# Ordering the first score product of pairs 2 to 5 behind the values of the pair two places ahead

## The chip, the cores and the metric

The kernel runs on one core of a Trainium2 chip. The metric is the device time of one execution in microseconds (us), the median of several runs. The engines are TensorE (PE: matrix products, with the loads of its stationary operand shown apart as PEld), VectorE (DVE), ScalarE (ACT) and GpSimd (POOL); SyncE (SP) issues the DMA transfers. Each engine works through its own queue in order and waits on semaphores for the others.

## The reference

Attention with a compressive memory, followed by a feed-forward block with the Mish activation (names shortened):

```python
def _attn_ref(q, k, v, M_prev, z_prev, beta):          # q, k, v: (4, 8, 576, 64)
    scores = q @ k.T / sqrt(D), causal mask             # per batch and head
    a = exp(scores - scores.max(-1)); a /= a.sum(-1) + 1e-09
    local = a @ v
    q_p = where(q > 0, q, exp(q) - 1) + 1
    mem_out = (q_p @ M_prev) / (q_p @ z_prev + 1e-06)
    g = sigmoid(beta)                                   # per head
    return g * mem_out + (1 - g) * local

def reference(...):
    x = attn_out.transpose(0, 2, 1, 3).reshape(2304, 512)
    h = x @ w_in                                        # (512, 2048)
    return (h * tanh(softplus(h))) @ w_out              # (2048, 512)
```

All data are float32.

## The kernel before

**Pairs.** The 4 x 8 heads are handled as 16 pairs of heads, numbered 0 to 15. For each pair `load`, `load2` and `loadv` bring q and k transposed (`f`), q by rows (`qn`), `z` and `v` (with M_prev as its first 64 rows). Then come:

- `scores(p)`: the scores of both heads in four products, held in the list `banks`: `(4, 0, 288)` means query tile 4 against keys 0 to 287. The query tiles have up to 128 rows; tile 4 has all 576 keys and takes two products, `(4, 0, 288)` and `(4, 288, 576)`. Each product goes into a PSUM tile `s`; up to pair 3 there are two of these in turn, later one. DVE masks each piece and takes its running extreme in one instruction (`ttr`, L388, into the row buffer `w` and `mx`); the masking of keys 288 to 575 needs the extreme of keys 0 to 287. ACT takes the exponential with its sum (L395).
- `prep(p)`: the feature map of q (`p0`, exponential, `ph2`), its product with z on POOL and the denominators on DVE (L346 to L351).
- `norm(h)`: the reciprocal of the row sums (L431, L434), the scaling of the rows by it on POOL (L95), and the memory part, written into the same row buffer (POOL, L89).
- `transp(h)`: 15 transposes of 128 x 128 on PE (L459) in four groups, each evicted from PSUM into `at` (L112 on ACT, L114 on DVE, in turn: ACT, DVE, ACT, DVE).
- `av(p)`: the values, two groups of products (L487) into one accumulator `vps`; each group is copied by ACT (`xo`), and DVE subtracts the copy from the accumulator (`xl`, L89) to keep the rounding remainder. The second group needs the first one's accumulator free and all four evictions of both heads. `put` stores both to DRAM (`xs`).

**Weights.** The feed-forward weights are 16 column tiles, split into two float32r parts each. `split(...)` makes for one tile two conversions (`narrow`): a load into `raw`, a scaling on ACT (L93), on DVE L158, L164, L167 and L174, a cast on ACT, a subtraction on POOL and the last addition on DVE (L89, into `wi` or `wo`). Six tiles are converted in the attention part, after the scores of pairs 1 (one), 3 (one), 4 (two), 5 (one) and 6 (one); `raw` has one buffer there. The rest follows after the attention.

**Feed-forward part.** `steps_a` makes products for 9 blocks of 256 tokens with the six tiles already converted: L237 (input products, into `h`), Mish and a split, then L253 (output products, into `acc`). From pair 4 on some of these steps are put into the program behind each pair. `tail` does the remaining tiles for all tokens (L580, L597).

**What sets the order.** The program is written pair by pair, but the framework's scheduler deals the instructions out to the engine queues by priorities (`run(..., name)` shifts them by the table `OFF`) and by a timeline of its own. `order_after(ins, first)` (L99) adds a dependency without a semaphore: `ins` must stand behind `first` on its engine. `queued` (L105) uses it to keep the values of a pair in order; `before[0]` is the last values product so far.

Of the kernel before, what the change touches and what calls it, by code (L numbers as in the profile page):

```python
# [51 lines left out]
def f32(ap):  # L52
    return ap.bitcast(F32)
# [25 lines left out]
def attention_moe_kernel(ctx: ExitStack, tc: tile.TileContext, f_src, qn, vn, zz, beta, w_in, w_out, out):  # L79
    nc = tc.nc  # L80
# [7 lines left out]
    def tt(name, **kw):  # L88
        engines[ENG[name]].tensor_tensor(**kw)  # L89
# [7 lines left out]
    before = [None]  # L97

    def order_after(ins, first):  # L99
        tc.add_manual_dep(  # L100
            ins.ins, first.ins.name,
            mybir.DependencyInfo(mybir.DependencyClass.NoSync, mybir.DependencyReason.DATA), reason="order",
        )

    def queued(ins, chain):  # L105
        if chain:
            order_after(ins, before[0])
        before[0] = ins

    def copy(which, o, i):  # L110
        if which == "a":
            nc.scalar.copy(out=o, in_=i)  # L112
        elif which == "v":
            nc.vector.tensor_copy(out=o, in_=i)  # L114
        else:
            nc.gpsimd.tensor_scalar(out=o, in0=i, scalar1=1.0, scalar2=1.0, op0=ALU.mult, op1=ALU.mult)
# [161 lines left out]
    def attention():  # L278
# [9 lines left out]
        ps_v = st.enter_context(tc.tile_pool(name="ps_v", bufs=1, space=PS))  # L288

        pr = {}  # L290
        hd = {}
        turn = {"t": 0, "s": 0}
        early = ExitStack()
# [2 lines left out]
        def spare(p, order, pool, tag, shape):  # L296
            if p < EARLY and order[turn[tag] % len(order)] == "e":
                pool = ps_e
            turn[tag] += 1
            return pool.tile(shape, F32, tag=tag, name=tag)  # L300
# [56 lines left out]
        def scores(p):  # L357
            f = pr[p]["f"]
            gs = [hd.setdefault(2 * p + e, {}) for e in range(2)]
            ops = []  # L360

            def begin():
                for g in gs:
                    g["w"] = rp.tile([128, 1920], F32, tag="w", name="w")
                    g["mx"] = sp.tile([128, 6], F32, tag="mx", name="mx")
                    g["sm"] = sp.tile([128, 5], F32, tag="sm", name="sm")

            def mms(bank):
                ps = spare(p, SQ, ps_s, "s", [128, 2, 512])
                for e, g in enumerate(gs):  # L370
                    g["ps"] = ps[:, e]
                o = 0
                for m, a, b in bank:
                    n = b - a
                    q0 = QT[m][0]
                    for e, g in enumerate(gs):
                        le = slice(64 * e, 64 * e + 64)
                        nc.tensor.matmul(  # L378
                            g["ps"][:, o:o + n], f[le, 0, q0:q0 + 128], f[le, 1, a:b], start=True, stop=True
                        )  # L380
                    o += n

            def ttr(g, m, a, b, o):
                n = b - a
                c0 = 448 + (a - (QT[m][1] - 128)) if m else 448
                mx = g["mx"]
                acc = mx[:, 5:6] if b == 288 else mx[:, m:m + 1]
                nc.vector.tensor_tensor_reduce(  # L388
                    out=g["w"][:, WO[m] + D + a:WO[m] + D + b], in0=g["ps"][:, o:o + n], in1=mask[:, c0:c0 + n],
                    scale=-E_SC, scalar=3.0e38 if a == 0 else mx[:, 5:6], op0=ALU.add, op1=ALU.min, accum_out=acc,  # L390
                )

            def exp(g, m):
                row = g["w"][:, WO[m] + D:WO[m] + D + QT[m][1]]
                nc.scalar.activation(  # L395
                    out=row, in_=row, func=ACTF.Exp, scale=-1.0, bias=g["mx"][:, m:m + 1], accum_out=g["sm"][:, m:m + 1]
                )

            ops.append(begin)
            for bank in banks:  # L400
                ops.append(lambda bank=bank: mms(bank))
                for g in gs:
                    o = 0
                    for m, a, b in bank:
                        ops.append(lambda g=g, m=m, a=a, b=b, o=o: ttr(g, m, a, b, o))
                        o += b - a
                    for m, a, b in bank:
                        if b != 288:
                            ops.append(lambda g=g, m=m: exp(g, m))
            return ops  # L410
# [62 lines left out]
        def av(p):  # L473
            d = pr[p]
            at = [hd[2 * p + e]["at"] for e in range(2)]

            def mms(j):
                if j == 0:
                    d["xo"] = tp.tile([128, S], F32R, tag="xo", name="xo", bufs=2)
                    d["xl"] = tp.tile([128, S], F32, tag="xl", name="xl", bufs=2)  # L480
                q0, ops = AVJ[j]
                n = ops[0][2]
                ps = g_["v", j] = ps_v.tile([128, n], F32, tag="v", name="vps")
                last = len(ops) - 1
                for k, (t, a, b, gi, c) in enumerate(ops):
                    for e in (1, 0):
                        queued(nc.tensor.matmul(  # L487
                            ps[64 * e:64 * e + 64, a:b], d["v"][:, t, e], at[e][gi][:, c:c + b - a],
                            start=(k == 0), stop=(k == last),
                        ), k or e == 0)  # L490

            def cp(j):
                q0, n = AVJ[j][0], AVJ[j][1][0][2]
                xo = d["xo"][:, q0:q0 + n]
                copy("a", xo, g_["v", j][:])
                tt("xlo", out=d["xl"][:, q0:q0 + n], in0=g_["v", j][:], in1=f32(xo), op=ALU.subtract)

            def put():
                b, c = divmod(p, 4)
                nc.sync.dma_start(out=xs[b][:, 0, c, :], in_=f32(d["xo"][:]))  # L500
                nc.sync.dma_start(out=xs[b][:, 1, c, :], in_=d["xl"][:])

            g_ = {}
            ops = []
            for j in range(2):
                ops += [lambda j=j: mms(j), lambda j=j: cp(j)]
            return ops + [put]

        load(0)
        nc.sync.dma_start(out=gt[:, 2, :], in_=beta.to_broadcast([128, H]))  # L510
# [10 lines left out]
        for p in range(NP):  # L521
            load2(p)
            loadv(p)
            if p + 1 < NP:
                load(p + 1)
            run(scores(p), 'scores')
            run(prep(p), 'prep1')
            for _ in range(CV.get(p, 0)):
                run(split(wst, cp, nf), 'conv')
                nf += 1  # L530
            for e in range(2):
                run(norm(2 * p + e), 'norm')
                run(transp(2 * p + e), 'transp')
            run(av(p), 'av')
            if p == EARLY - 1:
                early.close()
                open_banks(st)
            if p >= P0:
                if (p - P0) % 4 == 0:
                    todo.extend(steps_a((p - P0) // 4))  # L540
                n = int(SPREAD * (p - P0 + 1)) - done[0]
                for _ in range(n):
                    run([todo.pop(0)], 'p1')
                done[0] += n
        st.close()

    def tail(mlist):
# [68 lines left out]
        st.close()  # L616

    attention()
    for k in range((NP - P0) // 4, (NA + 1) // 2):
        todo.extend(steps_a(k))  # L620
# [63 lines left out]
```

## Time and profile before

| | |
|---|---|
| median of 3 runs | 658.97 us (657.48 to 659.05) |
| profiled execution: time / span | 658.83 us / 657.0 us |
| PE busy, share of the span | 598.3 us, 91% |
| DVE busy | 334.2 us, 51% |
| ACT busy | 299.6 us, 46% |
| POOL busy | 170.3 us, 26% |
| mean granted PE clock | 0.966 of full |

The span runs from the first to the last instruction of the profiled execution; its time has 1.8 us more around it. Busy times are unions over an engine's instructions. The attention part takes the first 340 us or so, its second half mixed with feed-forward products; the last 250 us are feed-forward alone. A line with "[1.36 <-ACT xo L112]" means that the engine idled 1.36 us before it and that ACT's instruction at L112 which writes `xo` ended the wait.

### The profile page before, as it was taken

The page shows a single profiled execution, that of the slowest core. Times are in us where ns is not written, and L with a number is a line of the kernel's source. Part 1 is how long each engine was busy: PE and PEld are TensorE (multiplying, and loading weights), DVE is VectorE, ACT ScalarE, POOL GpSimd, SP SyncE. Part 2 cuts the span into 40 slices and gives each one's busy share as a digit, 9 for nine tenths or more (in the row PEclk, how much of TensorE's full clock was granted, in tenths as well). Part 3 has the DMA queues.
Part 4 walks back from the last instruction along what each step waited for, and adds up shares of the span by engine and source line. Part 5 has one row for each costly group of instructions (what it writes and reads, how often), then busy time and mean ns, then how long its engine had stood idle before and what let it go on. Part 6 is the DMA issues. An engine that isn't in the chain of part 4 may idle for free.

```text
span 657.0 us, 9863 instructions
## 1 busy us (share of the span) xinstructions
PE 598.3 (91%) x3488; PEld 470.3 (72%) x3488; DVE 334.2 (51%) x900; ACT 299.6 (46%) x688; POOL 170.3 (26%) x260
## 2 busy tenths in 40 slices
PE   3578868989988999989998999999999999999997
PEld 2345535767755877668887978888888888888886
DVE  4989887884575664635237888920311211121121
ACT  3677645866665775746244544621222222222221
POOL 3697885565435444414000000000000000000000
PEclk9579976999998999999998999999999999999999
DMA  6345566314545324421157666404302220430220
GB/s 227 98 137 159 191 208 213 127 58 144 167 149 187 97 86 129 155 105 58 50 178 245 215 235 208 128 1 128 111 19 71 90 95 1 129 128 1 64 97 32
DMA packets 50913, 80.86 MB, mean 123 GB/s; under 512 B 8112, under 2 KB 26544, under 8 KB 50864
## 3 DMA queue, kind: packets, MB, share of 16 engines
q1 hardware_dynamic: 50864, 80.24, 37.6%
q8 instruction: 27, 0.44, 0.3%
q14 instruction: 22, 0.18, 0.1%
HBM read 61.35 MB, written 18.87 MB: 122 GB/s over the span
## 4 chain that ended last, share of the span: by engine, by line
PE 50%; DMA 5%; DVE 2%; ACT 2%; issue 1%; POOL 1%; SPq 0%; DVEq 0%; ACTq 0%
PE o L597 19%; PE h L580 19%; PE h L237 5%; PE acc L253 4%; DMA raw<-in_w_in_dram 3%; PE vps L487 2%; PE t L459 2%; DMA part<-ob 1%; PE s L378 1%; POOL w L95 0%; DMA qn<-in_qn_dram 0%; DVE ws L174 0%; DVE wa L164 0%; ACT w L395 0%; ACT wa L93 0%
## 5 line engine op out<-in xcount | busy, mean ns | idle before, releaser
L89 DVE TENSOR_TENSOR g<-u,g 128x512 fp32r<-128x512 f32 (+1 forms) x77 | 50.7, 666 | 190.2 <-ACT g L112 190.1
L580 PE MATMUL h<-xb,wi 128*128 128x512 f32 (+1 forms) x600 | 134.8, 368 | 0.0
L597 PE MATMUL o<-wo,g 128*128 128x512 f32 x540 | 133.8, 390 | 0.0
L219 ACT ACTIVATE u<-h 128x512 f32<-128x512 f32 (+1 forms) x77 | 42.8, 569 | 180.9 <-PE h L580 168.5
L580 PEld LDWEIGHTS h<-xb,wi 128*128 128x128 f32 x600 | 106.0, 188 | 19.6
L597 PEld LDWEIGHTS o<-wo,g 128*128 128x128 f32 x540 | 100.6, 188 | 20.3
L95 POOL TENSOR_SCALAR w<-w,rc 128x64 f32<-128x64 f32 (+4 forms) x160 | 95.3, 617 | 72.8 <-ACT w L395 31.9
L395 ACT ACTIVATE w<-w,mx 128x576 f32<-128x576 f32 (+4 forms) x160 | 88.3, 553 | 31.0 <-DVE mx L388 30.4
L378 PE MATMUL s<-f 64*128 64x288 f32 (+4 forms) x384 | 69.2, 472 | 35.9 <-DVE mx L388 29.6
L237 PE MATMUL h<-xb,wi 128*128 128x256 f32 x648 | 93.5, 292 | 4.6 <-ACT u L219 4.6
L237 PEld LDWEIGHTS h<-xb,wi 128*128 128x128 f32 x648 | 83.7, 194 | 9.4 <-ACT u L219 5.4
L459 PE MATMUL t<-ident,w 128*128 128x128 f32 x480 | 77.1, 290 | 8.7 <-ACT at L112 5.9
L253 PE MATMUL acc<-wo,g 128*128 128x512 f32 x324 | 82.0, 396 | 0.6 <-ACT u L219 0.6
L378 PEld LDWEIGHTS s<-f 64*128 64x128 f32 x384 | 35.8, 209 | 62.2 <-DVE mx L388 37.5
L459 PEld LDWEIGHTS t<-ident,w 128*128 128x128 f32 x480 | 54.8, 146 | 27.6 <-issue 10.2
L253 PEld LDWEIGHTS acc<-wo,g 128*128 128x128 f32 x324 | 58.9, 188 | 12.7 <-ACT u L219 0.8
L487 PE MATMUL vps<-at,v 128*64 128x256 f32 (+2 forms) x512 | 62.2, 386 | 4.9 <-DVE at L114 2.7
L388 DVE CUSTOM_DVE_ANT_0 w<-s,mask 128x288 f32<-128x288 f32 (+4 forms) x160 | 59.3, 420 | 12.6 <-PE s L378 12.6
L487 PEld LDWEIGHTS vps<-at,v 128*64 128x64 f32 x512 | 35.8, 144 | 30.4 <-issue 6.4
L114 DVE COPY at<-t 128x448 f32<-128x448 f32 x64 | 41.6, 650 | 15.4 <-PE t L459 15.4
L112 ACT CAST g<-u 128x512 fp32r<-128x512 f32 (+1 forms) x77 | 44.8, 594 | 1.6
L93 ACT ACTIVATE wa<-raw 128x512 f32<-128x512 f32 x32 | 21.8, 681 | 43.2 <-DMA raw<-in_w_in_dram 18.6
(45 smaller groups left out, 445.3 us busy)
## 6 DMA issues: line engine op xcount, KB each, us to landing
f<-in_f_src_dram SPq DMA_DIRECT2D x32, 288.0 KB, 4.2
xb<-xs SPq DMA_DIRECT2D x36, 256.0 KB, 4.6
raw<-in_w_in_dram SPq DMA_DIRECT2D x16, 512.0 KB, 3.6
raw<-in_w_out_dram SPq DMA_DIRECT2D x16, 512.0 KB, 3.8
qn<-in_qn_dram SPq DMA_DIRECT2D x16, 320.0 KB, 3.1
v<-in_vn_dram SPq DMA_DIRECT2D x16, 320.0 KB, 3.3
xs<-xo SPq DMA_DIRECT2D x16, 288.0 KB, 3.2
xs<-xl SPq DMA_DIRECT2D x16, 288.0 KB, 3.4
```

The lines of the kernel that those rows point to most:

```text
L89: engines[ENG[name]].tensor_tensor(**kw)
L95: engines[which].tensor_scalar(out=o, in0=i, scalar1=scale, scalar2=1.0, op0=ALU.mult, op1=ALU.mult)
L112: nc.scalar.copy(out=o, in_=i)
L237: ins = nc.tensor.matmul(ps[:, TA * a:TA * a + TA], wi[y, f][:, c, :], x[c][:, z], start=(q == 0), stop=(q == 11))
L253: nc.tensor.matmul(acc[:], g[:, y, c:c + 128], wo[z, f], start=(f == 0 and y == z), stop=(f == KA - 1 and z == 1),)
L378: nc.tensor.matmul(g["ps"][:, o:o + n], f[le, 0, q0:q0 + 128], f[le, 1, a:b], start=True, stop=True)
L388: nc.vector.tensor_tensor_reduce(out=g["w"][:, WO[m] + D + a:WO[m] + D + b], in0=g["ps"][:, o:o + n], in1=mask[:, c0:c0 + n], scale=-E_SC, ...
L395: nc.scalar.activation(out=row, in_=row, func=ACTF.Exp, scale=-1.0, bias=g["mx"][:, m:m + 1], accum_out=g["sm"][:, m:m + 1])
L459: nc.tensor.transpose(ps[:, o:o + 128], g["w"][:, c:c + 128], ident[:])
L487: queued(nc.tensor.matmul(ps[64 * e:64 * e + 64, a:b], d["v"][:, t, e], at[e][gi][:, c:c + b - a], start=(k == 0), stop=(k == last),), k o ...
L580: nc.tensor.matmul(ps[:, :n], wi[a, f][:, c, :], x[c][:, b], start=(k == 0), stop=(k == 11))
L597: nc.tensor.matmul(D_[t][:], g[:, y, 128 * t:128 * t + 128], wo[z, f], start=(f == KA and y == z), stop=(f == NF - 1 and z == 1),)
```

## The change

The first score product of a pair, `(4, 0, 288)`, of both its heads, is ordered on PE behind the last values product of the pair two places ahead, for pairs 2 to 5. `av` records that product when its operations have been issued.

```diff
+        last_av = {}
...
-                        nc.tensor.matmul(
+                        ins = nc.tensor.matmul(
                             g["ps"][:, o:o + n], f[le, 0, q0:q0 + 128], f[le, 1, a:b], start=True, stop=True
                         )
+                        if a == 0 and m == 4 and 2 <= p < 6:
+                            order_after(ins, last_av[p - 2])
...
-            return ops + [put]
+            return ops + [put, lambda: last_av.update({p: before[0]})]
```

No operation is added. The scheduler's queues differ up to pair 13 on all engines; the lists below show three places. Line numbers of the changed kernel are 3 higher there (L379 is its score product, L462 its transpose, L490 its values, L391 its masking); names keep their numbers.

PE, early in the attention part: `v_154` are the values of pair 0, `w_321` the rows of pair 1's first head and `w_324` of its second, `f_504` the q and k of pair 3, `f_318` of pair 2. Before:

```order
L459 MATMUL t_415<-ident_102,w_321 128x128 x4
L378 MATMUL s_675<-f_504 128x288 x2
L459 MATMUL t_422<-ident_102,w_321 128x128 x4
L459 MATMUL t_429<-ident_102,w_321 128x128 x4
L378 MATMUL s_680<-f_504 128x288 x2
L487 MATMUL vps_297<-at_279,v_154 64x256
```

Now:

```order
L490 MATMUL vps_297<-at_265,v_154 64x128
L490 MATMUL vps_297<-at_228,v_154 64x128
L379 MATMUL s_513<-f_318 128x288 x2
L462 MATMUL t_446<-ident_102,w_324 128x128
L462 MATMUL t_452<-ident_102,w_324 128x128 x2
```

Before, pair 3's first two score products stood ahead of the second values group of pair 0. Now that group comes first, then pair 2's first score product; pair 3's come after the values of pair 1. Pair 2's second product, which has no such edge, stands ahead of pair 0's values.

DVE, at the values of pair 4: `at_1030` is the last DVE eviction of that pair's transposed rows, `xl_1038` its remainder; `ws_1163` belongs to the fifth converted tile, `wa_1426` and `ws_1427` to the last conversion of the sixth. Before:

```order
L114 COPY at_1030<-t_1031 128x512
L167 TENSOR_SCALAR ws_1163<-wa_1162 128x512
L434 RECIPROCAL rc_1185<-rc_1185 128x5
L351 RECIPROCAL den_1655<-den_1655 128x10
L434 RECIPROCAL rc_1222<-rc_1222 128x5
L89 TENSOR_TENSOR xl_1038<-vps_1039,xo_1037 128x320
L174 SCALAR_TENSOR_TENSOR ws_1163<-raw_1161,ws_1163 128x512
```

Now:

```order
L164 SCALAR_TENSOR_TENSOR wa_1426<-wa_1426,ws_1427 128x512
L391 ISA w_1360,mx_1361<-s_1366,mask_103 128x288
L391 ISA mx_1361 128x1
L391 ISA w_1363,mx_1364<-s_1366,mask_103 128x288
L391 ISA mx_1364 128x1
L167 TENSOR_SCALAR ws_1427<-wa_1426 128x512
L174 SCALAR_TENSOR_TENSOR ws_1427<-raw_1425,ws_1427 128x512
L89 TENSOR_TENSOR xl_1038<-vps_1039,xo_1037 128x320
L114 COPY at_1030<-t_1031 128x512
```

Before, the eviction stood ahead of the rest of the fifth tile's conversion and of all of the sixth's but its first part's beginning; now all but one step of both tiles stand ahead of it.

PE, behind the values of pair 7: `vps_1744` are these values, `f_1839` the q and k of pair 9, `w_1842` and `w_1845` the rows of pair 8, `acc` the output products of the feed-forward part. Before:

```order
L487 MATMUL vps_1744<-at_1675,v_1601 64x128
L378 MATMUL s_2089<-f_1839 128x320 x2
L378 MATMUL s_2089<-f_1839 128x192 x2
L459 MATMUL t_1926<-ident_102,w_1842 128x128 x4
L459 MATMUL t_1943<-ident_102,w_1845 128x128 x3
```

Now:

```order
L253 MATMUL acc_2017<-wo1_5_101,g_1785 128x512
L253 MATMUL acc_1995<-wo1_5_101,g_1785 128x512
L462 MATMUL t_1926<-ident_102,w_1842 128x128 x4
L379 MATMUL s_2089<-f_1839 128x320 x2
L379 MATMUL s_2089<-f_1839 128x192 x2
L462 MATMUL t_1943<-ident_102,w_1845 128x128 x3
```

The two `acc` rows are the last of 20 that now stand between pair 7's values and the last score product of pair 9, with the third score product of pair 9 and ten transposes of pair 8 (four of these before).

## Rows read from the trace of the kernel before

**Rows 1.** The page, part 1: busy us, share of the span, instructions.

```profile
PE 598.3 (91%) x3488; PEld 470.3 (72%) x3488; DVE 334.2 (51%) x900; ACT 299.6 (46%) x688; POOL 170.3 (26%) x260
```

**Rows 2.** Timeline of PE: start, us, what; second values groups of pairs 4, 7, 8, 9, 13.

```profile
110.58 2.17 PE L487 MATMUL vps<-at,v 128*64 128x256 f32 x20
...
186.27 2.17 PE L487 MATMUL vps<-at,v 128*64 128x256 f32 x20
...
200.46 2.17 PE L487 MATMUL vps<-at,v 128*64 128x256 f32 x20
...
214.76 2.17 PE L487 MATMUL vps<-at,v 128*64 128x256 f32 x20
...
300.35 2.17 PE L487 MATMUL vps<-at,v 128*64 128x256 f32 x20
```

**Rows 3.** Busy times by stretch: stretch, length, engines (instructions), PE clock, DMA share, GB/s.

```profile
39.15:116.40 77.25, 61.64 (x413) 39.62 (x414) 68.63 (x212) 47.88 (x131) 59.50 (x81) 0.85 0.56 181
...
112.74:143.14 30.40, 27.14 (x200) 21.18 (x201) 24.32 (x59) 22.64 (x47) 20.77 (x26) 1.00 0.33 111
143.14:188.44 45.30, 44.55 (x295) 33.05 (x294) 26.64 (x92) 27.48 (x68) 19.98 (x31) 1.00 0.39 129
188.44:216.92 28.48, 22.71 (x161) 14.19 (x161) 19.04 (x70) 17.77 (x54) 15.33 (x29) 0.94 0.53 175
216.92:284.04 67.12, 64.74 (x462) 49.42 (x462) 35.54 (x126) 44.70 (x105) 25.82 (x46) 1.00 0.38 118
284.04:302.52 18.48, 16.61 (x113) 11.47 (x113) 9.82 (x41) 11.43 (x37) 5.95 (x12) 1.00 0.23 79
```

The engines stand in the order PE, PEld, DVE, ACT, POOL.

**Rows 4.** Waits of DVE, 39.15 to 116.4 us: us in total, times, longest.

```profile
DVE xl L89 <- ACT xo L112: 3.6, 2, 2.2
DVE den L346 <- POOL phe L89: 2.6, 2, 1.9
DVE ws L158 <- DMA raw<-in_w_out_dram: 1.6, 1, 1.6
DVE ws L158 <- DMA raw<-in_w_in_dram: 0.8, 1, 0.8
```

**Rows 5.** Timeline of DVE at the values of pair 4.

```profile
107.42 0.68 DVE L114 COPY at<-t 128x512 f32<-128x512 f32 x1
...
110.03 0.49 DVE L89 TENSOR_TENSOR xl<-vps,xo 128x320 f32<-128x320 f32 x1 [1.36 <-ACT xo L112]
```

**Rows 6.** Groups of DVE by form, 39.15 to 116.4 us: count, busy us, mean ns, idle before.

```profile
L164 DVE SCALAR_TENSOR_TENSOR wa<-wa,ws 128x512 int32<-128x512 int32 x7 | 5.1, 728 | 0.0
...
L174 DVE SCALAR_TENSOR_TENSOR ws<-raw,ws 128x512 f32<-128x512 uint32 x6 | 4.9, 811 | 0.0
...
L158 DVE TENSOR_SCALAR ws<-raw 128x512 int32<-128x512 int32 x7 | 3.5, 503 | 2.4 <-DMA raw<-in_w_out_dram 1.6 <-DMA raw<-in_w_in_dram 0.8
L167 DVE TENSOR_SCALAR ws<-wa 128x512 int32<-128x512 int32 x6 | 3.3, 557 | 0.0
L89 DVE TENSOR_TENSOR wo<-wa,ws 128x512 fp32r<-128x512 f32 x3 | 3.0, 1003 | 0.0
...
L89 DVE TENSOR_TENSOR wi<-wa,ws 128x512 fp32r<-128x512 f32 x3 | 1.9, 646 | 0.0
```

**Rows 7.** The page, part 6: DMA issues, KB each, us from issue to landing.

```profile
raw<-in_w_out_dram SPq DMA_DIRECT2D x16, 512.0 KB, 3.8
```

**Rows 8.** The page, part 5: groups of PE, busy us and mean ns of one.

```profile
L459 PE MATMUL t<-ident,w 128*128 128x128 f32 x480 | 77.1, 290 | 8.7 <-ACT at L112 5.9
L253 PE MATMUL acc<-wo,g 128*128 128x512 f32 x324 | 82.0, 396 | 0.6 <-ACT u L219 0.6
```

**Rows 9.** Timeline of PE between the values of pairs 7 and 9: score groups.

```profile
188.61 1.13 PE L378 MATMUL s<-f 64*128 64x320 f32 x8 [0.17 <-DVE mx L388]
...
193.46 0.76 PE L378 MATMUL s<-f 64*128 64x288 f32 x4 [2.47 <-DVE mx L388]
...
208.32 0.76 PE L378 MATMUL s<-f 64*128 64x288 f32 x4 [1.84 <-DVE mx L388]
```

## What it should do to the time

> **What bounds the kernel now.** Start with the totals of the page. TensorE (PE) is busy for 91% of the span and VectorE (DVE) for 51% [rows 1], but this is a mean over stages with different limits. So read next the busy times by stretch, which I cut where PE ends the values of one pair: pair 4 at 112.75 us, pair 7 at 188.44, pair 8 at 202.63, pair 9 at 216.93, pair 13 at 302.52 [rows 2]. (These ends are start plus length of the second values group of each pair.) The stretches [rows 3] show three regimes. From 39.15 to 116.40 us DVE works 68.63 of 77.25 us, PE 61.64 with its clock at 0.85 of full on the mean. There DVE is the limit. From 143.14 to 188.44 PE is busy 44.55 of 45.30 us and DVE only 26.64: PE is the limit, since the products of the feed-forward part fill it. From 188.44 to 216.92 the queue holds none of these, PE idles 28.48 - 22.71 = 5.8 us, and the chain of one pair (scores, mask, exponential, scaling, transposes, values) sets the pace. From pair 13's last transposes on, the PE queue of the changed kernel is the same as before, instruction by instruction, and so are the other queues from a little before or after. So the whole effect is how much later or earlier the values of pair 13 end; the remaining 355 us move with them.
>
> **The profiled execution** took 658.83 us, 1.8 us more than its span of 657.0, and stands 0.14 us under the median of the runs (658.97). A measurement of this kernel can tell about 0.3% (2 us) from no change. The sum below is made against 658.83.
>
> **What the edit does.** It adds no operation and no DMA. It puts one score product of each of four pairs behind the values of the pair two places ahead, and the scheduler, which fills the queues by its own timeline, then deals out all that follows anew: PE, DVE, ScalarE, GpSimd and the DMA queue differ up to pair 13. Each of the four edges itself costs nothing, as both ends are on PE. What counts is what moved.
>
> **Step 1, up to the values of pair 4.** Nothing here was late because of pair 0's values; DVE is the limit, and its queue now holds more ahead of the point that matters. The values of pair 4 need the fourth DVE eviction of that pair's transposed rows, at 107.42 to 108.10 us before [rows 5]. In the new order 21 DVE instructions stand ahead of it that stood behind, and none goes the other way. Three are reciprocals and one is a subtraction that pair 4's values wait for in either order. The other 17 are steps of the weight conversion: by their mean times [rows 6] four of L167 (0.557), four of L174 (0.811), three of L158 (0.503), three of L164 (0.728), two last additions into wi (0.646) and one into wo (1.003), which is 2.23 + 3.24 + 1.51 + 2.18 + 1.29 + 1.00 = 11.5 us; about 11.9 with the small ones. Before, the values started at 110.58, 2.5 us after the eviction, because the subtraction that frees their accumulator came later (110.03 + 0.49 us) [rows 2, 5]. In the new order the eviction comes last: it would end at 108.10 + 11.9 = 120.0, and the values 2.2 us later at 122.2 instead of 112.75: **+9.5 us**, if DVE idles in all as long as before.
>
> That "if" is the main unknown. DVE's idle time in this stretch is 8.6 us: 3.6 behind the copies of the values, 2.6 behind GpSimd's product for the denominators, 2.4 behind loads of raw weights [rows 4]; of it 5.6 us lie ahead of the eviction (all but 1.36 us before the subtraction [rows 5] and the 1.6 us behind a raw load, which come after it). From below: if the new order closed all these gaps, step 1 would be 9.5 - 5.6 = +4. From above: the raw tile has one buffer for the conversions of this stage, a load lands 3.8 us after its issue [rows 7], and three more loads fall into the stretch; if each is waited for as long as the worst one was (1.6 us), it is 9.5 + 4.8 = +14. I take one more such wait of middle size (2.4 / 2 = 1.2): **+10.7**. This is nearer to the upper rows, because the new DMA order also puts loads of the feed-forward part, which wait for stores of pairs 2 and 3, ahead of raw loads on the one queue. GpSimd gets the same instructions; its scaling of pair 2's rows now stands behind its product with z for pair 4, and what it idles there DVE covers.
>
> **Step 2, from pair 4 to pair 7.** PE is the limit. At the end of pair 7's values the new order has done less: 20 output products of the feed-forward part now stand behind it (82.0 / 324 = 0.253 us each [rows 8], 5.1 us), with six transposes (77.1 / 480 = 0.16 us each [rows 8], 1 us) and a score group of pair 9 (the next one took 1.13 [rows 9]). That is **-7** for this stretch, and only a loan. A true gain is that the conversions are over before it starts: DVE was busy 24.32 of 30.40 us in its first part, and PE idled 3.3 + 0.75 = 4.0 us in both parts [rows 3]. Between nothing and all 4.0 I take half, **-2**, since the larger waits of PE here are for masked scores, which wait for DVE only in part. Pair 7 then ends at +10.7 - 7 - 2 = +1.7 us.
>
> **Step 3, from pair 7 to pair 9.** The 7 us of loaned work come back in the stretch where PE idled 5.8 us. If they fell into that idle time alone, the cost would be 7 - 5.8 = +1.2; if they all came on top, +7. The order says where they are: in front of pair 9's last score product, which before started at 188.61, right behind pair 7's values, and 28.3 us before pair 9's values ended [rows 2, 9]. It now starts 7 to 8 us later. Not all of that is passed on, because PE also waited 2.47 and 1.84 us for masked scores of pairs 10 and 11 there [rows 9], and these waits give way. I take the middle, rather below: **+3.5**.
>
> **Step 4, from pair 9 to pair 13.** Here the second portion of output products is done earlier: 19 of them (4.8 us) lay between the values of pairs 12 and 13 and now lie ahead of pair 12's end, where PE is full (64.74 of 67.12 us [rows 3]). Without this filler the last pair needs what pair 9 needed after pair 8, 216.93 - 202.63 = 14.3 us [rows 2], instead of 18.48 [rows 3]: 4.8 - 4.2 = **+0.6** (0 to 2).
>
> **Sum:** 1.7 + 3.5 + 0.6 = +5.8 us, so 658.83 + 5.8, about **664.5 us**. All low ends together give 4 - 7 - 4 + 1.2 = -5.8 (653), all high ends 14.3 - 7 + 7 + 2 = +16 (675).
>
> One rule speaks against this change more strongly. Rows 3 show a regime that DVE limits followed by one that PE limits, with conversions in both; the change draws the conversions together in the first. The Trainium skill, page "Perfetto Trace Analysis", section "Optimization Strategy", says that where the most contended engine changes over time, interleaving the regimes may help. By that rule the move is a loss of the whole 11.5 us of conversion and little returns, some 670 us; by the rows the holes give part of it back.
>
> **The rivals.**
> - *Faster.* DVE closes its gaps, because pair 0 and 1 are evicted earlier and the conversions give it something to do while scores are late. Step 1 is then +4, step 2 gives back its whole 4.0 us and the loaned work fits into the hole (+1.2): 653 to 656 us. It decides if DVE's idle time ahead of pair 4's last eviction falls from 5.6 us to under some 2. For it: a fourth to a third of all DVE idle time is behind GpSimd and could be covered. Against it: the new order adds a stage in which DVE must wait for pair 2's first scores behind pair 0's values. Chance 0.22.
> - *No change that can be told.* Step 1 stays near +8 and the hole swallows the loaned work: 8 - 7 - 2 + 1.2 + 0.6 = +0.8, so 659 to 660 us. For it: 5.8 us of idle PE [rows 3]. Chance 0.17.
> - *Much slower.* Raw loads stand behind feed-forward loads on the DMA queue, DVE waits for them with all its other work behind, and pair 9's chain passes on its whole delay: step 1 +14, step 3 +7: 668 to 675 us. Chance 0.15.
> - *It does not do what it says.* Only the first product of a pair has the edge. In pair 2 the second product is now first on PE, ahead of pair 0's values, and holds one of the two score buffers until the first has been masked. This costs nothing by itself, as the third product needs that buffer's partner, and it has no chance of its own.
>
> **How the numbers follow.** The forecast, +3 to +9 us, has 0.46. Slower by over 0.3% is 0.46 + 0.15 = 0.61, within 0.3% 0.17, faster 0.22. The range leaves out the better half of the faster case and the worst third of the much slower one: 655 to 672 us. The likeliest case's own range is 661 to 668.
>
> **What would show it.** In the changed profile the second values group of pair 4 should end near 123 us (right), not near 113; DVE should be some 88% busy from 39 us to there, and at most one conversion step should come between it and the end of the attention part. Pair 7's values should end at 188 to 192, pair 9's near 222, and the stretch from pair 13 on should keep its length within 1 us. I am wrong in step 1 if pair 4 ends before 118, in step 3 if pair 9 ends less than 29 us after pair 7, and altogether if the time after pair 13 changes.

## The result and the profile after

The changed kernel takes **666.59 us** (median of 4 runs, 666.43 to 667.41) against 659.01 of the kernel before in the same comparison (4 runs, 657.48 to 660.39): ratio 1.0124, 95% interval 1.0102 to 1.0146. It is slower, by 7.6 us where 5.8 were forecast. The profiled execution took 666.43 us, its span 664.6 us, 7.6 more than before. Of a later run (e5, below) one execution took 1163 us, with TensorE's products 1.7 times as long; it is in no number here.

The page, part 1, of the change (to read with [rows 1]):

```profile
PE 605.3 (91%) x3488; PEld 475.9 (72%) x3488; DVE 341.3 (51%) x900; ACT 301.6 (45%) x688; POOL 162.3 (24%) x260
```

The totals hardly tell the two kernels apart; the stretches do. First the busy times of the kernel before, cut at the ends of the values of pairs 4, 7, 9 and 13 (columns as in [rows 3]: length, busy time of PE, PEld, DVE, ACT and POOL, PE clock, DMA share, GB/s; its stretch from pair 7 to pair 9 stands there):

```profile
39.15:112.74 73.59, 57.98 (x385) 36.55 (x385) 66.57 (x208) 45.76 (x127) 55.84 (x76) 0.84 0.55 176
112.74:188.44 75.70, 71.69 (x493) 54.23 (x493) 50.96 (x150) 50.12 (x115) 40.75 (x57) 1.00 0.37 122
...
216.92:302.52 85.60, 81.35 (x574) 60.89 (x573) 45.36 (x164) 56.12 (x141) 31.77 (x58) 1.00 0.35 110
302.52:657.00 354.48, 346.18 (x1801) 294.04 (x1801) 125.30 (x227) 110.17 (x202) 5.53 (x10) 0.99 0.33 106
```

The same stretches of the change, which answer to [rows 3]:

```profile
39.15:130.15 91.00, 65.73 (x392) 41.74 (x393) 77.58 (x220) 49.77 (x134) 58.89 (x82) 0.76 0.49 155
...
130.15:195.05 64.90, 63.79 (x458) 49.10 (x458) 39.73 (x126) 45.61 (x104) 28.14 (x50) 1.00 0.38 120
195.05:227.91 32.86, 28.94 (x195) 19.43 (x195) 21.58 (x78) 18.58 (x55) 15.86 (x29) 0.95 0.52 161
227.91:311.06 83.15, 81.32 (x573) 60.56 (x573) 48.67 (x165) 56.93 (x140) 32.82 (x59) 1.00 0.36 113
...
298.47:311.06 12.59, 12.15 (x92) 7.78 (x92) 9.40 (x35) 8.61 (x27) 5.94 (x12) 1.00 0.29 91
311.06:664.60 353.54, 346.28 (x1801) 294.10 (x1801) 125.85 (x227) 110.34 (x202) 5.53 (x10) 0.99 0.33 106
```

Up to pair 4 the change loses 91.00 - 73.59 = 17.4 us. From pair 4 to pair 7 it wins 75.70 - 64.90 = 10.8 back, loses 4.4 to pair 9 (32.86 against 28.48), wins 85.60 - 83.15 = 2.45 from there to pair 13, and 0.9 after it (the row from 298.47 us is the last pair of that stretch alone): 17.4 - 10.8 + 4.4 - 2.45 - 0.9 = +7.6.

Where do the 17.4 us come from? DVE, up to the end of the last DVE eviction of pair 4, before and after (the rows are of two kernels):

```profile
39.15:108.10 68.95, 53.34 (x354) 33.99 (x356) 63.29 (x197) 44.25 (x123) 51.70 (x70) 0.85 0.57 186
```
```profile
39.15:127.92 88.77, 63.56 (x371) 40.32 (x371) 76.70 (x217) 48.15 (x130) 56.66 (x78) 0.76 0.50 158
```

DVE does 76.70 - 63.29 = 13.4 us more work ahead of that point and idles 12.1 us instead of 5.7, 6.4 more. Its waits in the change, up to there (us in total, times, longest; they answer to [rows 4]):

```profile
DVE ws L158 <- DMA raw<-in_w_out_dram: 6.1, 2, 5.1
DVE xl L89 <- ACT xo L112: 4.5, 3, 2.3
```

The long one stands alone in the timeline of DVE, and the DMA queue's timeline shows why:

```profile
102.01 0.08 DVE L391 DVE_READ_ACCUMULATOR2_ANT mx<- 128x1 f32 x1
107.16 1.02 DVE L158 TENSOR_SCALAR ws<-raw 128x512 int32<-128x512 int32 x1 [5.06 <-DMA raw<-in_w_out_dram]
108.09 0.51 DVE L391 CUSTOM_DVE_ANT_0 w<-s,mask,mx 128x288 f32<-128x288 f32 x1
```
```profile
99.62 1.40 SPq L207 DMA_DIRECT2D xb<-xs  x3
101.12 0.41 SPq L154 DMA_DIRECT2D raw<-in_w_out_dram  x1
101.60 1.52 SPq L207 DMA_DIRECT2D xb<-xs  x3
```

The raw load is issued at 101.12, between two groups of three feed-forward loads, and its reader starts 6.0 us later (3.8 us was the load's median [rows 7]). Masking stands behind that reader on DVE. ScalarE waits for the same load, for 6.60 us, with an eviction of PE's transposes behind it, and PE idles 3.26 us until that eviction:

```profile
107.22 0.66 ACT L93 ACTIVATE wa<-raw 128x512 f32<-128x512 f32 x1 [6.60 <-DMA raw<-in_w_out_dram]
107.78 0.46 ACT L112 COPY at<-t 128x384 f32<-128x384 f32 x1
108.39 1.09 PE L462 MATMUL t<-ident,w 128*128 128x128 f32 x4 [3.26 <-ACT at L112]
```

The kernel before has a raw load in the same place among such loads, and its reader also starts late, 103.42 - 97.78 = 5.6 us after the issue. But there DVE had 4.8 us of other work ahead of it. Its queues of DMA and DVE:

```profile
96.28 1.39 SPq L207 DMA_DIRECT2D xb<-xs  x3
97.78 0.41 SPq L154 DMA_DIRECT2D raw<-in_w_in_dram  x1
98.23 1.46 SPq L207 DMA_DIRECT2D xb<-xs  x3
```
```profile
103.42 0.43 DVE L158 TENSOR_SCALAR ws<-raw 128x512 int32<-128x512 int32 x1 [0.82 <-DMA raw<-in_w_in_dram]
```

At pair 4 the eviction is now the last thing, as forecast: it is the DVE copy, and the second values group starts right behind it ([rows 2] and [rows 5] show the reverse order before).

```profile
127.25 0.67 DVE L114 COPY at<-t 128x512 f32<-128x512 f32 x1
```
```profile
127.98 2.17 PE L490 MATMUL vps<-at,v 128*64 128x256 f32 x20 [0.60 <-DVE at L114]
```

### The profile page after: what moved, and what is told of

It is laid out like the page before. It is cut to its first block, busy times and chain, and to the rows that moved or that the text cites. A ratio compares the mean times of both kernels' runs of the same rounds, so it can differ in the third digit from the quotient of the medians.

```text
span 664.6 us, 9849 instructions
## 1 busy us (share of the span) xinstructions
PE 605.3 (91%) x3488; PEld 475.9 (72%) x3488; DVE 341.3 (51%) x900; ACT 301.6 (45%) x688; POOL 162.3 (24%) x260
## 4 chain that ended last, share of the span: by engine, by line
PE 55%; DMA 5%; DVE 4%; ACT 2%; issue 1%; SPq 0%; POOL 0%; DVEq 0%; ACTq 0%
PE o L600 18%; PE h L583 18%; PE h L237 6%; PE acc L253 4%; DMA raw<-in_w_in_dram 4%; PE vps L490 3%; PE t L462 3%; PE s L379 2%; ACT w L398 1%; DMA xs<-xo 1%; DVE ws L174 1%; DVE w L391 1%; DVE wa L164 1%; DMA qn<-in_qn_dram 0%; ACT L219 0%
## 5 line engine op out<-in xcount | busy, mean ns | idle before, releaser
L89 DVE TENSOR_TENSOR g<-u,g 128x512 fp32r<-128x512 f32 (+1 forms) x77 | 53.3, 699 | 192.4 <-ACT g L112 192.4
L95 POOL TENSOR_SCALAR w<-w,rc 128x64 f32<-128x64 f32 (+4 forms) x160 | 88.7, 579 | 75.2 <-ACT w L398 35.1
L379 PE MATMUL s<-f 64*128 64x288 f32 (+4 forms) x384 | 73.1, 495 | 31.1 <-DVE mx L391 24.7
L237 PE MATMUL h<-xb,wi 128*128 128x256 f32 x648 | 91.2, 291 | 5.0 <-ACT u L219 5.0
L462 PE MATMUL t<-ident,w 128*128 128x128 f32 x480 | 82.3, 305 | 12.5 <-ACT at L112 7.4
L462 PEld LDWEIGHTS t<-ident,w 128*128 128x128 f32 x480 | 59.4, 154 | 33.2 <-issue 14.3
L379 PEld LDWEIGHTS s<-f 64*128 64x128 f32 x384 | 37.5, 219 | 58.0 <-DVE mx L391 32.4
L490 PE MATMUL vps<-at,v 128*64 128x256 f32 (+2 forms) x512 | 61.4, 383 | 6.8 <-DVE xl L89 4.0
L391 DVE CUSTOM_DVE_ANT_0 w<-s,mask 128x288 f32<-128x288 f32 (+4 forms) x160 | 59.3, 423 | 10.5 <-PE s L379 10.5
L490 PEld LDWEIGHTS vps<-at,v 128*64 128x64 f32 x512 | 35.2, 143 | 31.8 <-issue 5.1
L112 ACT COPY at<-t 128x384 f32<-128x384 f32 x64 | 33.6, 525 | 29.3 <-PE t L462 29.3
```

The costliest lines, as they stand in the source:

```text
L95: engines[which].tensor_scalar(out=o, in0=i, scalar1=scale, scalar2=1.0, op0=ALU.mult, op1=ALU.mult)
L237: ins = nc.tensor.matmul(ps[:, TA * a:TA * a + TA], wi[y, f][:, c, :], x[c][:, z], start=(q == 0), stop=(q == 11))
L379: ins = nc.tensor.matmul(g["ps"][:, o:o + n], f[le, 0, q0:q0 + 128], f[le, 1, a:b], start=True, stop=True)
L391: nc.vector.tensor_tensor_reduce(out=g["w"][:, WO[m] + D + a:WO[m] + D + b], in0=g["ps"][:, o:o + n], in1=mask[:, c0:c0 + n], scale=-E_SC, ...
L462: nc.tensor.transpose(ps[:, o:o + 128], g["w"][:, c:c + 128], ident[:])
L490: queued(nc.tensor.matmul(ps[64 * e:64 * e + 64, a:b], d["v"][:, t, e], at[e][gi][:, c:c + b - a], start=(k == 0), stop=(k == last),), k o ...
```

## The experiments

The theories, as the expectations call them. **A**: the conversions that the new order draws ahead of pair 4's last DVE eviction (42 of 60 DVE steps stood there before, 59 in the change) are the loss. **B**: score products that are held back cost by themselves, first of all those of pair 2. **C**: the waits of DVE for the one raw buffer are the loss. **D**: TensorE's lower granted clock (0.76 of full to pair 4, 0.84 before) is the loss. "Pair 4 at +17" says how much later than in the kernel before pair 4's values end.

### Conversions moved, without any edge on the scores (e2, e8)

Drawn ahead (59 steps), in the kernel before:

```diff
-CV = {1: 1, 3: 1, 4: 2, 5: 1, 6: 1}
+CV = {1: 1, 3: 1, 4: 4}
...
-            nc.vector.scalar_tensor_tensor(
+            hold[0] = nc.vector.scalar_tensor_tensor(
...
+                    if h == 9 and base == 3:
+                        order_after(ins, hold[0])
```

> The kernel before, without any score edge, but with the conversions of all four later tiles issued with pair 4 and ordered on DVE ahead of its last eviction: 59 steps ahead of it instead of 42. Theory A: pair 4's values end 12 to 17 us later than before, as in the change, and the whole takes 664 to 668 us. Theory B: no score is later, so pair 4 ends at most 5 us later and the whole takes 658 to 662 us.

Measured: 670.29 us against 660.24, ratio 1.0155 (1.0111 to 1.0199). Pair 4 at +25.3 and pair 13 at +9.8. Held back (20 steps), also in the kernel before:

```diff
-CV = {1: 1, 3: 1, 4: 2, 5: 1, 6: 1}
+CV = {1: 1, 3: 1, 5: 3, 6: 1}
...
+            if hold[0] is not None:
+                order_after(ins, hold[0])
...
+                hold[0] = last_ev[9] if nf >= 2 else None
```

> The opposite of the change on DVE: no edge on the scores; of the conversions of this stage the last ones (from the third tile on) are put behind the last DVE eviction of pair 4, so that 20 steps stand ahead of it (42 before, 59 in the change). Theory A: pair 4's values end up to 22 x 0.65 = 14 us earlier, as far as DVE and not the chain of scores is the limit there; 99 to 107 us. What this is worth at the end: 653 to 657 if the conversions then hide beside the feed-forward products, 660 or more if they come into the stretch between pairs 7 and 9, as in the run that held back the tiles 5 and 6 in the change.

Measured: 656.12 us against 658.44, ratio 0.9964 (0.994 to 0.9989). Pair 4 at -10.4, pair 7 at -11.9, pair 9 at -1.9, pair 13 at -4.4. The stretch to pair 4 in both, e2 first:

```profile
39.15:138.07 98.92, 64.76 (x412) 39.93 (x413) 82.39 (x246) 54.31 (x151) 73.89 (x97) 0.80 0.48 152
```
```profile
39.15:102.36 63.21, 54.17 (x404) 35.52 (x404) 53.86 (x185) 42.10 (x122) 49.02 (x78) 0.95 0.53 170
```

DVE's busy time goes 53.86, 66.57, 82.39 us with 20, 42 and 59 steps ahead, and the stretch goes 63.21, 73.59, 98.92 us with it. The stretch gives up 10.4 us for 12.7 us less work, and takes 25.3 for 15.8 more. So without the edges A holds in both directions. In e2 the effect is larger than A expected (12 to 17 us at pair 4, 664 to 668 in all): 9.5 of the 25.3 us are more idle time of DVE, 3.3 of it inside the conversions, where one last addition waits for the subtraction on GpSimd. And it is partly a loan in both: of 25 us some 10 are left at pair 13, of 10 gained some 4.

### Conversions held back in the change (e1, e9)

The same `order_after` at L158 in the changed kernel: in e1 for the last two converted tiles (`nf >= 4`, 40 steps ahead of the eviction, the table `CV` as before), in e9 with exactly the lines of e8 (20 steps).

> The changed kernel with the conversions of the fifth and sixth weight tile ordered on DVE behind the last eviction of pair 4's transposed rows: 40 conversion steps stand ahead of that eviction, against 59 in the change and 42 before. Theory A (conversions drawn ahead of pair 4 on the limiting engine, with the raw load they wait for): the 17.4 us by which pair 4's values end later shrink to 0 to 6 us, and the whole takes 658 to 662 us. Theory B (scores placed later starve the chain of pairs 2 to 4): pair 4 still ends 12 us or more late, and the whole stays at 664 to 668 us.

Measured: 676.53 us against 660.24, ratio 1.0238 (1.0212 to 1.0264). Pair 4 at +8.5, half of the change's lateness, but pair 5 at +13.0 and pair 13 at +14.5: nothing is given back. The time lies above the ranges of both theories (658 to 662 and 664 to 668).

> The change with its four edges, and with the same holding back of conversions that made the kernel before 2.3 us faster (656.1): from the third tile on they stand behind pair 4's last DVE eviction, 20 steps ahead of it instead of 59. If the loss of the change comes only through the conversions that it draws ahead (theory A), the edges now cost nothing: pair 4's values end at 102 to 106 us, and the whole takes 655 to 658. If the later score products cost by themselves as well (the single edges gave +5 to +7 us by their medians, with 41, 42 and 51 steps ahead; theory B), it takes 660 to 664, and pair 4's values end 5 us or more after those of that kernel (102.4).

Measured: 671.68 us against 658.82, ratio 1.0216 (1.018 to 1.0252). Pair 4 at +1.1, pair 7 at -4.1, pair 8 at +18.6. Here too the time lies above both ranges (655 to 658 and 660 to 664). The stretches to pairs 4 and 9, and DVE's waits in the first:

```profile
39.15:113.83 74.68, 56.83 (x392) 36.76 (x392) 52.42 (x183) 39.89 (x118) 45.49 (x76) 0.89 0.44 144
...
184.29:230.95 46.66, 40.07 (x233) 27.36 (x232) 24.46 (x81) 26.38 (x68) 17.68 (x31) 0.93 0.43 136
```
```profile
DVE phe L332 <- DMA qn<-in_qn_dram: 9.8, 3, 5.4
DVE xl L89 <- ACT xo L114: 5.4, 4, 1.9
DVE at L116 <- PE t L466: 3.6, 4, 1.5
DVE w L395 <- PE s L383: 2.1, 2, 1.3
```

DVE has less work than in e8 (52.42 against 53.86 us) and yet pair 4 comes 113.83 - 102.36 = 11.5 us later: DVE idles 22.3 us there, and 9.4 in e8. It waits for loads of `qn`, for values, for transposes and for scores. So A alone is not the whole: with the edges other waits lie close behind DVE's work, and taking the work away bares them. How many of them the later scores cause (B) is not shown. The largest item, 9.8 us for `qn`, points elsewhere: the longest of these waits is for a load issued behind six feed-forward loads, as the raw load of the change stood behind three.

```profile
95.06 2.93 SPq L211 DMA_DIRECT2D xb<-xs  x6
98.03 0.47 SPq L317 DMA_DIRECT2D qn<-in_qn_dram  x1
```
```profile
103.64 0.49 DVE L332 TENSOR_SCALAR phe<-qn 128x640 f32<-128x640 f32 x1 [5.37 <-DMA qn<-in_qn_dram]
```

With conversions held back, both runs lose time behind pair 4: e1 takes 34.95 us from pair 4 to pair 5 (30.40 before [rows 3]), and in e9 pair 7 to pair 9 takes 46.66 us instead of 28.48, with 40.07 us of PE work in it where 22.71 stood before [rows 3]. So taking the conversions away brings pair 4 back, but not the whole time: both runs are slower than the change.

### One edge at a time (e3, e7, e6)

```diff
-                        if a == 0 and m == 4 and 2 <= p < 6:
+                        if a == 0 and m == 4 and p == 2:
```

and the same with `p == 3` (e7) and `p == 4` (e6). With the edges of pairs 2 to 4 alone the queues of all engines come out as in the change: the edge of pair 5 does nothing.

> Only the edge of pair 2 (its first score product behind pair 0's values), not those of pairs 3 and 4: 42 conversion steps ahead of pair 4's last eviction, as before. Theory A: pair 4 ends within 4 us of before, the whole 658 to 661 us. Theory B: pair 2's scores are as late as in the change, which already costs: pair 4 ends 6 us or more late, the whole 662 to 667 us.

> Only the edge of pair 3 is kept. 41 conversion steps stand ahead of pair 4's last DVE eviction (42 before), and pair 2's scores stand where they stood before. Theory A and theory B both say nothing is lost: pair 4's values end within 2 us of before, and the whole within 1.5 us of before. If it is slower by 3 us or more, a late score product costs by itself, in whichever pair it is, and neither theory is whole.

> Only the edge of pair 4 is kept. 51 conversion steps stand ahead of pair 4's last DVE eviction (42 before, 59 in the change), and pair 2's scores stand where they stood before. Theory A (conversions drawn ahead): pair 4's values end 9 x 0.65 = about 6 us later than before (some 118 to 120 us), and at the end 2 to 4 us are left: 661 to 664. Theory B (the later first scores of pair 2 are what costs, the rest is given back): pair 2's values end within 1 us of before, and the whole within 1.5 us of before.

Measured, with the conversion steps ahead of the eviction:

| edge | steps | pair 4 | pair 13 | time (before) | ratio, interval |
|---|---|---|---|---|---|
| pair 2 | 42 | +2.7 | +3.9 | 663.59 (660.24) | 1.0046 (1.003 to 1.0062) |
| pair 3 | 41 | +0.7 | +3.2 | 663.08 (658.44) | 1.007 (1.0045 to 1.0095) |
| pair 4 | 51 | +10.0 | +6.7 | 666.08 (658.44) | 1.0108 (1.0069 to 1.0147) |
| all | 59 | +17.4 | +8.5 | 666.59 (659.01) | 1.0124 (1.0102 to 1.0146) |

Two things follow. An edge that moves no conversion ahead still costs 3 to 5 us, more than A allowed (661 us at most for pair 2, within 1.5 us of before for pair 3). These runs too have other queues than the kernel before on every engine, so whether the held-back product itself costs this or what moved with it was not separated; B's sign for pair 2, a pair 4 that is 6 us late, did not come (+2.7). And the edge of pair 4 alone costs nearly as much as all of them: its nine steps more make pair 4 late by 10.0 us, where 6 were expected. The costs don't add. Why the edges of pairs 2 and 3 cost what they do was not settled beyond the place: in each of the two runs pair 4 to pair 7 takes longer than before (77.46 and 79.58 us against 75.70).

### Two raw buffers, in both kernels (e4, e5, e10, e11)

```diff
-            t["r"] = raw = pool.tile([128, 512, 2], I32, tag="raw", name="raw", bufs=1 if own is cp else RT)
+            t["r"] = raw = pool.tile([128, 512, 2], I32, tag="raw", name="raw", bufs=2 if own is cp else RT)
```

In the change:

> The change with a second buffer for the raw weights of the conversions in the attention part; 60 steps ahead of pair 4's last eviction. Theory C (the one wait of 5.1 us for a raw load is what made step 1 dearer than forecast): DVE waits for raw loads under 1.5 us ahead of pair 4's values, which end 4 to 6 us earlier than in the change, and the whole takes 661 to 664 us. Theory A without C: the steps are still ahead, pair 4 ends within 3 us of the change, the whole 665 to 668 us.

Measured: 662.61 us against 660.24, ratio 1.0034 (1.002 to 1.0048). The waits for raw tiles are gone from DVE's list, pair 4 is at +14.8 and pair 13 at +3.4. Pair 4 ends only 2.6 us earlier than in the change, where C expected 4 to 6, but the time is in C's range. C seems right, until the control is run, the same edit in the kernel before:

> The kernel before, without any edge, but with two buffers for the raw weight tile of this stage. It is the control for the run of the change with two buffers, which came 3.6 us under the change's own time. In its order 48 conversion steps stand ahead of pair 4's last DVE eviction (42 before). Theory C (the raw waits cost the kernel before 2.4 us in this stretch too, and they are on its path): 656 to 658.5 us with no wait for a raw tile left in the list of DVE's waits. Theory A (only the amount of DVE work ahead of pair 4's values counts: six more steps, 6 x 0.65 = +4 us at pair 4, half of it kept at the end): 659.5 to 662. If it stays within 1 us of before, the buffer mends only what the change spoils.

> The kernel before with two buffers for the raw tile once more, for a profile that can be read (that of the first run was taken while TensorE's products took nearly twice as long) and as a check on its 652.2 us. Theory C: 650 to 654 us; no wait of DVE for a raw tile between 39 and 122 us; pair 4's values end at 108 to 113, no later than before although six more conversion steps stand ahead of them. Otherwise the time should be back at 657 to 660.

Measured: 652.19 us against 658.44, ratio 0.9887 (0.9846 to 0.9928), and again 650.32 against 658.82, ratio 0.9882 (0.9847 to 0.9918). Both theories had expected less gain of e5 (656 to 658.5 and 659.5 to 662). The stretches to pair 4 and from there to pair 13, and PE's waits in the second, first of the kernel before:

```profile
39.15:112.33 73.18, 58.13 (x385) 36.38 (x385) 69.12 (x210) 45.85 (x129) 58.69 (x78) 0.86 0.57 183
112.33:295.61 183.28, 174.70 (x1231) 129.92 (x1231) 113.63 (x386) 123.72 (x311) 84.52 (x141) 0.99 0.39 124
```
```profile
PE s L378 <- DVE mx L388: 9.6, 9, 2.5
PE t L459 <- ACT at L112: 2.3, 5, 0.9
```
```profile
PE t L459 <- ACT at L112: 4.4, 3, 2.8
PE s L378 <- DVE mx L388: 2.7, 4, 1.1
```

Six more conversion steps stand ahead of pair 4's eviction (48), DVE does 2.55 us more there, but idles 4.1 us instead of 7.0, so pair 4 ends when it did. From pair 4 to pair 13 the time falls from 189.8 to 183.3 us; PE waited there 9.6 us for masked scores before, now 2.7. So the second buffer helps either kernel, by 0.9% (1.0034 / 1.0124) and 1.15% (0.9885, the mean of both runs); the intervals don't tell these two apart. The change costs no less with two buffers (1.0034 / 0.9885 = 1.015) than with one (1.0124). **C falls as the cause of the loss**; the waits are a cost that both kernels carry. The kernel before with two raw buffers beats both kernels of this case: the kernel before by 6.3 and 8.5 us in the two comparisons, and the change, across comparisons, by some 15 (652.19 or 650.32 against 666.59).

Both mends together, two buffers and the conversions of e8:

> Both mends on the kernel before: two buffers for the raw tile, and the conversions from the third tile on behind pair 4's last DVE eviction (20 steps ahead). If the two gains are of different waits they add: 652.2 - 2.3 = 650 us. If both take the same idle time, 652 or a little above. It is the candidate for a version that beats both kernels.

Measured: 653.91 us against 658.82, ratio 0.9936 (0.9914 to 0.9959): less gain than the buffer alone (650.32 in the same comparison). The gains don't add to the 650 us that two separate waits would have given. Pair 4 is at -7.0, but pair 7 to pair 9 takes 41.22 us, with 38.99 us of PE work in it (22.71 before [rows 3]), as in e9.

### More work for PE, to raise its clock (e12)

```diff
-                    nc.tensor.transpose(ps[:, o:o + 128], g["w"][:, c:c + 128], ident[:])
+                    for _ in range(2 if 4 <= h < 10 else 1):
+                        nc.tensor.transpose(ps[:, o:o + 128], g["w"][:, c:c + 128], ident[:])
```

> The change, with each transposition of pairs 2 to 4 issued twice into the same place: 90 more products on PE, 0.16 us each, 14 us of work that nothing needs, in the stretch where PE idles 25 us and its granted clock is 0.76 on the mean. 55 conversion steps stand ahead of pair 4's last DVE eviction (59 in the change). If the low clock is what makes pair 4 late (theory D), the clock there rises to 0.85 or more, pair 4's values end at 125 us or earlier, and the whole stays at 662 to 666. If DVE's work is the limit and the clock only follows from PE's idle time (theory A), pair 4's values stay within 2 us of 128 (four steps fewer than the change) and the whole at 665 to 669. If the added work lies on the chain itself: pair 4 at 133 or later, over 670.

Measured: 668.84 us against 658.82, ratio 1.0168 (1.013 to 1.0205).

```profile
39.15:130.21 91.06, 70.31 (x482) 48.80 (x482) 80.15 (x220) 50.06 (x134) 61.43 (x83) 0.86 0.49 158
```

The clock rises to 0.86, above that of the kernel before, and the stretch is as long as in the change (91.06 and 91.00 us). Of this 1.6 us are due to the last values group itself, which ran at the lower clock (3.81 us instead of 2.17); even without them D's 125 us are not reached (130.21 - 1.6 = 128.6). The run is not a clean one: the edit dealt out the queues anew (four conversion steps fewer, 2.6 us of DVE's waits for raw loads up to the eviction instead of 6.4), and the added work may hide a gain. What the change's own waits say is plainer. DVE waits for PE itself 0.6 us of its 12.1 up to the eviction, while most of PE's waits up to pair 4 end with DVE, the largest of them at the masking, before and after:

```profile
PE s L378 <- DVE mx L388: 8.5, 5, 3.3
```
```profile
PE s L379 <- DVE mx L391: 12.0, 6, 4.0
```

**D falls as the main cause**: the higher clock of e12 brought pair 4 no earlier, and DVE hardly waits for PE directly. That the low clock costs nothing at all is not shown.

## Why the prediction was right, step by step

The sign, the time (664.5 forecast, 666.6 measured) and the range were right. The mechanism that it named for the loss up to pair 4, a DVE queue with more conversions ahead of the eviction, is borne out there: by the rows of the change, by e2 and e8 without the edges, and by e9, where pair 4 is back at +1.1. It is not the whole of what the edges do, as e3 and e7 lose time without it. That the sum came within 1.8 us is luck: step 1 missed by +6.7 us, step 3 by +0.9, steps 2 and 4 by -1.8 and -3.05, and the time after pair 13 by -0.9. Of the signs the prediction set, pair 4 ended at 130.15 us (near 123 forecast), with DVE 85% busy to there (88), pair 7 at 195.05 (188 to 192) and pair 9 at 227.91 (222): all late by what step 1 had missed, in part given back.

- **Step 1 (+10.7, bounds +4 to +14) was mis-sized: +17.4**, beyond its upper end. Its signature came as told: pair 4's values wait for the DVE eviction, and at most one conversion step is left behind it. DVE's work ahead of the eviction grew by 13.4 us, where 11.5 to 11.9 were counted. The difference lies in operations that took longer; the clearest were in the stretch in either order. From the groups of DVE by form up to the eviction, before and after:

```profile
L431 DVE TENSOR_SCALAR rc<-sm,gt 128x5 f32<-128x5 f32 x9 | 2.6, 290 | 0.0
```
```profile
L434 DVE TENSOR_SCALAR rc<-sm,gt 128x5 f32<-128x5 f32 x9 | 4.8, 529 | 0.0
```

  The mean hides that most of the difference is two of the nine, with 1.5 us each (last section). The larger miss is DVE's idle time, +6.4 us where one wait of 1.2 was taken. One raw load alone is 5.06. The prediction priced each raw wait by the worst one of the kernel before, 1.6 us [rows 4], and blamed the place of the load on the queue for what might be added. But a load between feed-forward loads, 5.6 us from issue to reader, was there before; what had kept its wait at 0.82 us was other DVE work ahead of the reader, and that cover is what the new order takes away. (Its worth at pair 4 is less than its length: with two buffers the raw waits are gone, and pair 4 is 2.6 us earlier, e4.) The waits behind copies of the values grow too (4.5 us up to the eviction, 2.2 before), and those behind GpSimd (2.6 [rows 4]) are gone. With the 2.2 us from eviction to the end of the values (4.6 before), 13.4 + 6.4 - 2.4 = 17.4.
- **Step 2 (-9) was right: -10.8**, and so were its parts: PE's work in the stretch falls by 71.69 - 63.79 = 7.9 us (loan, 7 forecast), its idle time from 4.0 to 1.1 (2.9, 2 forecast).
- **Step 3 (+3.5) was right: +4.4.** 6.2 us of work come back (28.94 - 22.71), and the hole swallows 1.9 of them (idle 5.8 before, 3.9 after).
- **Step 4 (+0.6) failed in its sign: -2.45.** It said that the last pair without filler needs the 14.3 us that pair 9 needed. The rows show 12.59 us with 12.15 of PE work. PE's whole work from pair 9 to pair 13 is the same (81.3 us); its idle time falls from 4.2 to 1.8. The pairs up to pair 12 took 3.4 us more (4.8 forecast), the last one 5.9 less (4.2). Three other runs have the same 83.1 us, one of them without any edge (e4, e8, e9), so it is no accident of one execution.
- **After pair 13** 353.54 us against 354.48: unchanged within the 1 us allowed.
- **The rivals.** *Faster* needed DVE's idle time ahead of the eviction under 2 us; it is 12.1. *No change* needed step 1 near +8. *Much slower* came true in step 1, with a wait for a raw load and beyond its own +14, but not in step 3: the stretches behind pair 4 returned more than half. And one sentence under *It does not do what it says* was too quick. Pair 2's order "costs nothing by itself", it said, and each edge "itself costs nothing"; with pair 2's edge alone the kernel is 3 us slower (e3), by which wait is not shown.

The prediction set one rule of the Trainium skill beside this (page "Perfetto Trace Analysis", section "Optimization Strategy": interleaving regimes with different contended engines may help), which read against the change as 670 us. Without the edges the trace agrees with its direction: with fewer conversions in the stretch that DVE limits, the kernel is faster (0.9964 in e8); with more, slower (1.0155 in e2). With the edges it does not: with conversions held back the changed kernel was slower still (1.0238 in e1 and 1.0216 in e9, against 1.0124). The 670 us that the prediction drew from it are too much, since the stretches from pair 4 to pair 13 had 14.0 us of idle PE before (189.78 - 175.75 in the rows) and 6.9 after, which pay back 7 of the 17.

## What to carry to other kernels

When a dependency between two instructions of one engine lets a scheduler deal out everything anew, cost what moved, and split the time at a point where every queue must pass: work added in the stretch that DVE limits counted about in full or more there (10.4 us for 12.7 in e8, 17.4 for 13.4 in the change, 25.3 for 15.8 in e2), and part of it came back out of the idle time of the later stretches. Bound a wait for a load by its whole flight from issue to reader, not by the longest wait seen, since that one depends on the work that happened to cover it. And run the control: a mend that helps the slower kernel says nothing on why it is slower until the faster kernel has had it too.

## What was not expected of the hardware

- Of nine DVE operations on 128x5 elements two took 1.49 and 1.50 us in the change; six took 0.19 to 0.23 and one 0.47. Before, eight took 0.22 to 0.25 and one 0.81. Each of the three long ones ends within 0.04 us of the end of a GpSimd operation that began before it. The first two, with GpSimd's rows:

```profile
59.98 1.97 POOL L89 TENSOR_TENSOR phe<-qn,z 128x640 f32<-128x640 f32 x1
60.48 1.49 DVE L434 TENSOR_SCALAR rc<-sm,gt 128x5 f32<-128x5 f32 x1
...
74.43 1.91 POOL L89 TENSOR_TENSOR phe<-qn,z 128x640 f32<-128x640 f32 x1 [1.96 <-DVE qn L86]
74.88 1.50 DVE L434 TENSOR_SCALAR rc<-sm,gt 128x5 f32<-128x5 f32 x1
```

  That the one operation holds up the other is what the rows suggest; no run took the GpSimd operation away.
- TensorE's granted clock in the change was 0.50 of full (its 1.2 GHz level) from 100 to 110 us, after ten microseconds in which PE was busy 4.62, and 0.76 on the mean up to pair 4. With ninety more transposes the mean was 0.86, and pair 4's values ended no earlier (130.21 against 130.15).
